# Transformer block on one core: when FFN weights are loaded, how late broadcasts land in the planner's model, and the order of the prologue

## The chip, the cores and the metric

The kernel runs on one core of one Trainium2 chip. The time is device time of one launch in microseconds (us), the median of several runs. One launch under the profiler gives the trace from which all durations below are taken. Engines are named as in the profile: PE (TensorE matmul; PEld is its weight load), DVE (VectorE), ACT (ScalarE), POOL (GpSimd), SP (SyncE, which here only issues DMAs).

## What is computed

One transformer block with conditioned layer norms, 2048 tokens of width 512, 32 heads of width 16, a gated FFN of width 1792. Weights and activations are bf16.

```python
mod = (silu(c) @ w_mod).reshape(1, 6, 1, -1)      # sa, ca, ga, sb, cb, gb
h = layernorm(x) * (1 + ca) + sa
q, k, v = split(h @ wqkv)                         # 32 heads of 16
p = softmax(q @ k.T / 4)                          # per head, 2048 x 2048
x = x + ga * ((p @ v) @ wo)
h = layernorm(x) * (1 + cb) + sb
x = x + gb * ((gelu(h @ w_gate) * (h @ w_up)) @ w_down)
```

The scores of all heads have 32 x 2048 x 2048 elements, and each needs one exponential. That is the bulk of the work outside PE.

## The kernel before

**A recorder with a model of time.** The kernel is not written as a fixed list of instructions. While it is built, every operation goes through `rec` (L168), which finds its dependences, adds semaphore waits and books it in `model` (L245), an estimate of when each engine is free and when each result is there (`op.t1`). A transfer is there, by the model, 1600 ns after its issue, or when the transfers before it are through, plus its bytes at 350 B/ns, plus 1000 ns. `probe` (L274) asks when an operation could start. `stream` (L1033) uses these answers to put the operations of all engines in order: whatever can start soonest without holding up ACT goes next. The order within each engine is then fixed in the program; at run time an engine waits at an instruction whose inputs are not there, and so does all that is behind it on that engine. The places in the order thus depend on the model's times, and a change of any of them can move everything behind it.

**The stream.** Queries are cut into seven sets (`SETS`): two of 512 tokens, three of 256, two of 128. For every set there are eight units `qd` of four heads each. A unit is a row of items; an item is one bank of 512 score columns in PSUM (128 keys by 512 columns, or more keys by fewer queries). There are 2048 items in all, and `pos` counts them. PE writes the scores of three items (`qk`) into one half of six PSUM banks, and ACT takes the exponential of two or three banks in one instruction (E<-ps_sc, 1024 or 1536 columns). Some items go to DVE instead: `exp_vec` computes the exponential there in seven steps, one `dt<-ps_sc`, then `dx`, two multiplications and two scalings in f16 and a last combination. The planner gives an item to DVE only where the conditions at `if (('v', 3, 0) in self.have` hold, among them that fewer than `BACK` = 10 DVE steps are waiting and that DVE is free by its own model within 700 ns. PE then multiplies with V (`pv_round`, ps_pv<-E,vaug), where a column of ones in V also gives the sum of the exponentials.

**The reciprocals.** When a unit is through, `pv_done` copies the sums and outputs to SBUF (`osb`), marks the unit in `self.live`, and sends the denominators round: to DRAM (`da`, scr_den<-osb), back in 128 partitions (`db`, den<-scr_den), a reciprocal on DVE (`fin1`), to DRAM (`dc`, scr_rec<-rden), and back as a broadcast over 32 partitions for each of four heads (`dd`, rb<-scr_rec, 256 KB for a set of 512). `fin2` on DVE multiplies (onorm<-osb,rb) and takes the unit out of `self.live`. All four transfers are issued by SP, in program order, each after its wait. For the first two units, which are interleaved, both sets of transfers come close together. 47 broadcasts are made this way; the last four units get their reciprocals on PE and DVE.

**Side work.** While the exponentials run, PE, DVE and, for the tanh of GELU, ACT also do the projections of K, V and Q (`side_k`, `side_v`, `side_q`), the modulation columns (`side_mod`), the output projection (`side_wo`) and the FFN of the sets that are through (`side_ffn`). `plan` gives each its stretch of positions; a `credit` paces it. DVE steps are queued as `task`s; a task made by `evac` goes first.

**FFN weights.** `weight_parts` makes a list of twelve transfers of the FFN weights, 448 KB for w_gate and w_up and mostly 512 KB for w_down. In `stream`, each is issued on SP once the second modulation (`modB`) is there, one every eight positions (`loaded = pos + 8`). The last two parts of w_up lie where DVE keeps its exponentials in the first set, and are put back to the list after `ends[0]`. They are in SP's program order with the transfers of the reciprocals.

**The prologue.** In `prologue`, SP and ACT issue the first loads. ACT's queue has x tiles 0 and 1 (`x0`), then tiles 4 to 7 (`x2`, 512 KB), then two thirds of the first weight columns (`wq0`, `wq2`), then tiles 12 to 15 (`x4`). SP's queue has c, tiles 2 and 3 (`x1`), the first third of w_mod (`wm0`, 1 MB), `wq1`, tiles 8 to 11 (`x3`), the other columns of wqkv and the rest of w_mod. DVE computes mean and variance of tiles 0 to 3 (`ln_stat`: bn_stats and bn_aggr), POOL one power for all four (`ln_rstd(0, 4)`), DVE then normalises them. ACT sums tiles 4 and 5 (`act_stat`: a Copy and a Square, each with an accumulator), which three small DVE operations (`act_stat_fin`) turn into mean and variance. PE computes the modulation columns (`mod_cols`, which needs `wm0`), transposes the normalised tiles, and projects K and Q of the first 512 tokens, after which the first exponential can start. At its end the prologue does `ln_stat` of tiles 6 and 7. `side_first` then goes on with V of the first 512 tokens, and with layer norm, transposes, K and V of the other three groups of 512; group 1 (tiles 4 to 7) is the first of these.

Of the kernel before, what the change touches and what calls it, by code (L numbers as in the profile page):

```python
# [5 lines left out]
ACT = mybir.ActivationFunctionType  # L6
# [8 lines left out]
P = 128  # L15
S_TOK = 2048
D = 512
# [61 lines left out]
class _Recorder:  # L79
# [282 lines left out]
    def bn_aggr(self, out, in_):  # L362
        return self.rec("dve", lambda e: e.bn_aggr(out, in_), [in_], [out], cost=90)

    def dma(self, eng, out, in_, sem, noncontig=False):
        def fn(e):
            if noncontig:
                with self.nc.allow_non_contiguous_dma(reason="small strided transfer"):
                    return e.dma_start(out, in_)
            return e.dma_start(out, in_)  # L370
        n = mybir.dt.size(out.dtype)
        for _, k in out.ap:
            n *= int(k)
        return self.rec(eng, fn, [in_], [out], dma=sem, cost=n)

    def emit(self, final):
        for s in self.count:
# [34 lines left out]
class _Kernel(_Recorder):  # L412
# [12 lines left out]
    def alloc(self):  # L425
        sb, ps = self.sb, self.ps
        self.xs = sb("xs", [P, NT, D], BF16)
        self.qT = sb("qT", [P, NDC, S_TOK], BF16)
        self.km = [sb("kme", [P, NDC, S_TOK], BF16), sb("kmo", [P, NDC, S_TOK], BF16)]
        self.vaug = sb("vaug", [P, NKT, H * VW], BF16)  # L430
        hreg = sb("hreg", [P, NDC * S_TOK], BF16)
        self.hT = hreg[:, :].rearrange("p (a n) -> p a n", a=NDC)
        self.prodT = hreg[:, 0:NFC * 512].rearrange("p (f n) -> p f n", f=NFC)
        self.tb2 = hreg[:, 0:4 * D].rearrange("p (t n) -> p t n", t=4)
        wreg = sb("wreg", [P, NDC * 1536], BF16)
        self.wqkv = wreg[:, :].rearrange("p (a n) -> p a n", a=NDC)
        self.t2T = wreg[:, 0:NDC * 512].rearrange("p (a n) -> p a n", a=NDC)
        self.gw = wreg[:, 2048:6144].rearrange("p (b k n) -> p b k n", b=2, k=2)
        mreg = sb("mreg", [P, 2 * NDC * F], BF16)
        self.wmod = mreg[:, 0:NDC * 3072].rearrange("p (a n) -> p a n", a=NDC)  # L440
        self.wg = mreg[:, 0:NDC * F].rearrange("p (a n) -> p a n", a=NDC)
        self.wu = mreg[:, NDC * F:2 * NDC * F].rearrange("p (a n) -> p a n", a=NDC)
        dreg = sb("dreg", [P, NFC * D], BF16)
        self.wd = dreg[:, :].rearrange("p (f n) -> p f n", f=NFC)
        self.tb1 = dreg[:, 0:8 * D].rearrange("p (b t n) -> p b t n", b=2, t=4)
        self.warm = dreg[:, 8 * D:9 * D]
        self.wo = sb("wo", [P, 8, D], BF16)
        self.E = sb("E", [P, NSL, 512], BF16)
        self.dt = [sb("dt%d" % i, [P, 512], I32)[:, :] for i in range(ND)]
        self.dlo = [t.bitcast(U16).rearrange("p (n t) -> p n t", t=2)[:, :, 0] for t in self.dt]  # L450
        self.dx = [sb("dx%d" % i, [P, 512], FP16)[:, :] for i in range(ND)]
        own = [sb("ed%d" % i, [P, 512], BF16)[:, :] for i in range(NED - 4)]
        c = NDC * 3072
        self.ED = [own + [mreg[:, c + 512 * i:c + 512 * i + 512] for i in range(4)],
                   own + [self.qT[:, i, 0:512] for i in range(4)]]
        self.onorm = sb("onorm", [P, 8, 512], BF16)
        self.ga = sb("ga", [P, D], BF16)
        self.gb = sb("gb", [P, D], BF16)
        self.xw = sb("xw", [P, D], BF16)
        self.osb = sb("osb", [P, 1024], FP32)  # L460
        self.rb = sb("rb", [P, 1024], FP32)
        self.den = sb("den", [P, 4, 16], FP32)
        self.rden = sb("rden", [P, 4, 16], FP32)
        self.mv = sb("mv", [P, NT, 2], FP32)
        self.st6 = sb("st6", [P, 2, 6], FP32)
        self.rstd = sb("rstd", [P, NT], FP32)
        self.nwt = sb("nwt", [P, NT], FP32)
        self.crow = dreg[:, 9 * D:10 * D]
        self.tcol = sb("tcol", [P, NDC], FP32)
        self.asum = sb("asum", [P, 2, 6], FP32)  # L470
        self.half = sb("half", [P, 4], FP32)
        self.sc_bf = sb("sc_bf", [P, NDC], BF16)
        self.scbc = sb("scbc", [P, NDC, P], BF16)
        self.modA = sb("modA", [P, 8], FP32)
        self.modB = sb("modB", [P, 8], FP32)
        self.rm4 = sb("rm4", [P, 4], FP32)
        self.rm = sb("rm", [P, 2], FP32)
        self.ident = sb("ident", [P, P], BF16)
        self.ones = sb("ones", [P, P], BF16)
        self.self32 = sb("self32", [P, P], FP32)  # L480
        self.scp = ps("ps_sc", [P, SC, 512], FP32)
        self.pv = ps("ps_pv", [P, 512], FP32)
        self.mi = ps("ps_mi", [P, 512], FP32)
        self.scr1 = self.dram("scr_den", [4, 2048], FP32)
        self.scr2 = self.dram("scr_rec", [4, 2048], FP32)


    def prologue(self):
# [6 lines left out]
        self.dma(act, self.xs[:, 0:2, :], xv[:, 0:2, :], "x0")  # L495
        self.dma(sp, self.xs[:, 2:4, :], xv[:, 2:4, :], "x1")
        self.dma(sp, self.wmod[:, :, 0:1024], wmv[:, :, 0:1024], "wm0")
        self.dma(act, self.xs[:, 4:8, :], xv[:, 4:8, :], "x2")
        for k in range(3):
            self.dma(sp if k == 1 else act, wq4[:, :, k, 0:P], wqv[:, :, k, 0:P], "wq%d" % k)  # L500
        self.dma(sp, self.xs[:, 8:12, :], xv[:, 8:12, :], "x3")
        self.dma(act, self.xs[:, 12:16, :], xv[:, 12:16, :], "x4")
        for k in range(3):
# [20 lines left out]
            self.mm(self.scp[:, 0, dc:dc + 1], self.crow[0:1, P * dc:P * dc + P], self.ones[0:1, 0:1])  # L524
        self.warm_up(16)
        self.act(self.tcol[:, :], self.scp[:, 0, 0:NDC], ACT.Tanh, scale=0.5)
        for t in range(4, 6):
            self.act_stat(t)
        for t in range(2):
            self.ln_stat(t)  # L530
        self.stt(self.tcol[:, :], self.tcol[:, :], 1.0, self.scp[:, 0, 0:NDC], ALU.add, ALU.mult)
        self.ts(dve, self.sc_bf[:, :], self.tcol[:, :], 0.5, None, ALU.mult)
        for t in range(2, 4):
            self.ln_stat(t)
        self.ln_rstd(0, 4)
        self.mod_cols(self.scp[:, 1, 0:8], 0)
        self.warm_up(2)
        for t in range(4):
# [10 lines left out]
        self.act(self.km[0][:, 0, 0:512], bank, ACT.Copy, scale=self.rm[:, 0:1])  # L549
        self.proj_q(0, 0, self.scp[:, 4, :], dve)  # L550
        self.ts(dve, self.km[1][:, 0, 0:512], bank, self.rm[:, 1:2], None, ALU.mult)
        for t in range(6, 8):
            self.ln_stat(t)
        self.act_stat_fin(4, 6)

    def act_stat(self, t):
        self.act(self.xw[:, :], self.xs[:, t, :], ACT.Copy, accum=self.asum[:, 0, t - 4:t - 3])
        self.act(self.xw[:, :], self.xs[:, t, :], ACT.Square, accum=self.asum[:, 1, t - 4:t - 3])

    def act_stat_fin(self, a, b):  # L560
        m, q, t = self.asum[:, 0, a - 4:b - 4], self.asum[:, 1, a - 4:b - 4], self.nwt[:, a:b]
        self.ts("dve", self.mv[:, a:b, 0], m, 1.0 / D, None, ALU.mult)
        self.stt(t, m, 1.0 / D, self.mv[:, a:b, 0], ALU.mult, ALU.mult)
        self.stt(self.mv[:, a:b, 1], q, 1.0 / D, t, ALU.mult, ALU.subtract)

    def warm_up(self, n):
        for _ in range(n):
# [117 lines left out]
    def side_first(self):  # L685
        def stats(tiles):
            for t in tiles:
                self.task([lambda t=t: self.ln_stat(t)], ("st", t))

        def norms(t0):  # L690
            g = t0 // 4
            self.task([("pool", lambda: self.ln_rstd(t0, t0 + 4))]
                      + [lambda t=t: self.ln_norm(t0 + t, self.tb1[:, g % 2, t, :]) for t in range(4)], ("ln", g),
                      self.after([("st", t) for t in range(max(8, t0), t0 + 4)]))
        if not self.dry:
            norms(4)
        yield from self.side_v(0, 0)
        if not self.dry:
            stats([8, 9, 10, 11])
            norms(8)  # L700
            stats([12, 13, 14, 15])
        for g in range(1, 4):
            yield from self.until(("ln", g))
            for h in range(2):
                yield from self.side_t(("a", g), lambda t: self.tb1[:, g % 2, t, :], 4, h,
                                       lambda dc: self.hT[:, dc, 512 * g:512 * g + 512], self.modA)
            if g == 1 and not self.dry:
                norms(12)
            yield from self.side_k(g, 0)
            yield from self.side_v(g, 0)  # L710
# [322 lines left out]
    def stream(self):  # L1033
# [64 lines left out]
        while pos < nseq:  # L1098
            if pos >= ends[0] and all(rof[v] < rp for v in low):
                parts, late = parts + late, []  # L1100
            while parts and "modB" in self.have and pos >= loaded:
                parts.pop(0)()
                loaded = pos + 8
            t = max(self.pe_now(), virt)
# [171 lines left out]
    def pv_done(self, rnd, acc):  # L1276
# [20 lines left out]
        def fin1():  # L1297
            self.recip(rden, den)
            self.dma("sp", s2.rearrange("(p n) -> p n", p=P), rden, "dc%d" % sem)
            self.dma("sp", self.rb[:, lo:hi],  # L1300
                     s2.rearrange("(j o n) -> j o n", j=4, o=1).broadcast_to([4, 32, W]), "dd%d" % sem)

        def fin2():
            c = OCOL[sets[0]]
# [176 lines left out]
```

## Time and profile before

| | us |
|---|---|
| runs (three): median, lowest, highest | 906.48, 906.29, 910.97 |
| the profiled execution | 907.0 |
| its span, first to last instruction | 905.3 |
| busy in the span: ACT | 876.5 |
| busy in the span: DVE | 817.4 |
| busy in the span: PE | 796.2 |
| busy in the span: POOL | 16.2 |

The span leaves out 1.7 us that the time of the launch has around it. The granted clock is 1.000 throughout. The views of the profile give times from the span's start. In a row of the timeline, the brackets at its end show how long the engine sat idle before it and what ended that wait; rows are merged where the same group follows itself without a gap worth telling. In a row of waits stand the engine that waited, its result and line, what it waited for, the sum, the count and the longest. L320, L324, L332, L337, L341 and L307 are helpers (`act`, `tt`, `ts`, `stt`, `copy`, `mm`), so groups are told apart by the names of tiles, where a region has the name of its tensor: mreg and qT and ed also hold DVE's exponentials, wreg the FFN's gate, dreg w_down and the normalised tiles, hreg the transposed ones.

### The profile page before, as it was taken

How to read it: one execution, taken by the hardware profiler on the slowest of the kernel's cores; microseconds unless marked ns; L12 is line 12 of the kernel's file. 1: busy time of each engine (PE TensorE's matmuls, PEld its weight loads, DVE VectorE, ACT ScalarE, POOL GpSimd, SP SyncE). 2: the span in 40 equal slices, each digit the busy share in tenths (PEclk: the TensorE clock that was granted, in tenths of full speed). 3: DMA queues.
4: the chain of work that ended last, by engine and by line, in shares of the span. 5: the costliest groups of instructions: out<-in, count | busy, mean ns of one | idle time of the engine just before them, and what ended most of it. 6: DMA issues, size and time to landing. Idle time of an engine off the chain costs nothing.

```text
span 905.3 us, 20373 instructions
## 1 busy us (share of the span) xinstructions
PE 796.2 (88%) x8565; PEld 291.3 (32%) x8700; DVE 817.4 (90%) x1976; ACT 876.5 (97%) x744; POOL 16.2 (2%) x34
## 2 busy tenths in 40 slices
PE   8898988888888889888898888998888998998888
PEld 3333322322222222222233323333433343234455
DVE  7687999999998999999998999999899899978955
ACT  6999999999999999999999999999999999999993
POOL 2100000000000000000000000000000000000000
PEclk9999999999999999999999999999999999999999
DMA  9012220000100000000000000010000000000000
GB/s 302 2 25 90 84 71 13 14 14 13 54 14 4 11 13 14 14 4 23 19 26 14 9 14 11 11 32 14 14 14 14 20 14 8 27 14 9 17 19 13
DMA packets 32514, 25.15 MB, mean 28 GB/s; under 512 B 16233, under 2 KB 28262, under 8 KB 32422
## 3 DMA queue, kind: packets, MB, share of 16 engines
q1 hardware_dynamic: 30038, 22.27, 8.2%
q10 hardware_dynamic: 2384, 1.57, 0.6%
q8 instruction: 68, 1.11, 0.5%
q14 instruction: 24, 0.20, 0.1%
HBM read 21.23 MB, written 2.61 MB: 26 GB/s over the span
## 4 chain that ended last, share of the span: by engine, by line
ACT 74%; DVE 11%; PE 8%; DMA 5%; issue 1%; POOL 0%
ACT E L320 72%; PE ps_sc L307 4%; DMA rb<-scr_rec 4%; PE ps_mi L307 3%; ACT wreg L320 2%; DVE dt L332 2%; DMA scr_rec<-rden 2%; PE ps_pv L307 1%; DVE qT L332 1%; DVE dx L332 1%; DVE ed L324 1%; DVE ed L337 1%; DVE qT L324 1%; DVE qT L337 1%; DVE mreg L324 0%
## 5 line engine op out<-in xcount | busy, mean ns | idle before, releaser
L320 ACT ACTIVATE E<-ps_sc 128x1536 bf16<-128x1536 f32 (+2 forms) x698 | 849.2, 1425 | 12.5 <-PE ps_sc L307 12.1
L307 PE MATMUL ps_sc<-qT,kme 32*128 32x256 bf16 (+2 forms) x1600 | 170.2, 304 | 20.6 <-ACT E L320 13.2
L307 PE MATMUL ps_sc<-qT,kmo 32*128 32x256 bf16 (+2 forms) x1664 | 168.4, 298 | 17.3 <-ACT E L320 12.8
L307 PE MATMUL ps_pv<-E,vaug 128*17 128x256 bf16 (+2 forms) x2906 | 181.2, 300 | 1.7 <-DVE vaug L341 0.8
L332 DVE TENSOR_SCALAR dt<-ps_sc 128x512 int32<-128x512 f32 x189 | 129.8, 688 | 8.9 <-PE ps_sc L307 6.4
L307 PE MATMUL ps_sc<-kme,ident 128*128 128x512 bf16 x299 | 96.3, 384 | 39.0 <-ACT E L320 33.4
L307 PE MATMUL ps_mi<-wreg,mreg 128*128 128x256 bf16 (+2 forms) x605 | 115.8, 306 | 5.9 <-DVE wreg L337 2.2
L307 PEld LDWEIGHTS ps_sc<-qT,kme 32*128 32x128 bf16 x1600 | 48.9, 92 | 128.6 <-ACT E L320 73.9
L307 PEld LDWEIGHTS ps_sc<-qT,kmo 32*128 32x128 bf16 x1664 | 50.2, 92 | 119.3 <-ACT E L320 68.0
L307 PEld LDWEIGHTS ps_pv<-E,vaug 128*17 128x17 bf16 x2906 | 52.9, 88 | 97.7 <-issue 85.9
L324 DVE TENSOR_TENSOR qT<-qT,dx 128x512 f16<-128x512 f16 x190 | 77.9, 419 | 1.0
L332 DVE TENSOR_SCALAR dx<-dt 128x512 f16<-128x512 uint16 x189 | 77.2, 419 | 0.1
L307 PEld LDWEIGHTS ps_mi<-wreg,mreg 128*128 128x128 bf16 x624 | 48.7, 97 | 57.1 <-issue 26.5
L337 DVE SCALAR_TENSOR_TENSOR qT<-dt,qT 128x512 int16<-128x512 int32 x95 | 65.0, 685 | 0.5
L307 PE MATMUL ps_mi<-dreg,hreg 128*128 128x512 bf16 x179 | 56.8, 384 | 3.7 <-issue 2.2
L324 DVE TENSOR_TENSOR ed<-ed,dx 128x512 f16<-128x512 f16 x128 | 52.4, 419 | 0.5
L307 PEld LDWEIGHTS ps_sc<-kme,ident 128*128 128x128 bf16 x331 | 23.4, 97 | 88.5 <-ACT E L320 84.9
L337 DVE SCALAR_TENSOR_TENSOR ed<-dt,ed 128x512 int16<-128x512 int32 x64 | 43.7, 686 | 0.4
L341 DVE CAST wreg<-ps_mi 128x512 bf16<-128x512 f32 x51 | 35.1, 689 | 9.6 <-PE ps_mi L307 8.7
L307 PE MATMUL ps_mi<-hreg,wreg 128*128 128x512 bf16 x101 | 32.8, 384 | 4.7 <-DVE qT L332 2.5
L337 DVE SCALAR_TENSOR_TENSOR wreg<-wreg,ps_mi 128x512 bf16<-128x512 bf16 x51 | 34.8, 683 | 2.2 <-ACT wreg L320 1.1
L307 PE MATMUL ps_pv<-qT,vaug 128*17 128x256 bf16 (+2 forms) x166 | 36.1, 290 | 0.0
(130 smaller groups left out, 739.0 us busy)
## 6 DMA issues: line engine op xcount, KB each, us to landing
rb<-scr_rec SPq DMA_DIRECT2D x16, 256.0 KB
rb<-scr_rec SPq DMA_DIRECT2D x29, 128.0 KB
mreg<-in_w_mod_dram SPq DMA_DIRECT2D x1, 2048.0 KB, 14.4
out_dram<-xs SPq DMA_DIRECT2D x16, 128.0 KB, 1.7
mreg<-in_B_w_gate_dram SPq DMA_DIRECT2D x4, 448.0 KB, 7.6
mreg<-in_B_w_up_dram SPq DMA_DIRECT2D x4, 448.0 KB, 7.1
dreg<-in_B_w_down_dram SPq DMA_DIRECT2D x3, 512.0 KB, 7.0
wreg<-in_A_wqkv_dram SPq DMA_DIRECT2D x3, 384.0 KB, 10.6
```

What stands on the lines that cost most here:

```text
L307: return self.rec("pe", lambda e: e.matmul(out, lhsT, rhs, start=start, stop=stop, tile_position=tp), [lhsT, rhs], [out], cost=(n, int(rhs ...
L320: return self.rec("act", lambda e: e.activation(out, in_, func, scale=scale, **kw), rd, wr, cost=self.cost("act", out, [in_], "act" if bia ...
L324: return self.rec(eng, lambda e: e.tensor_tensor(out, a, b, op), [a, b], [out], cost=self.cost(eng, out, [a, b], "tt"))
L332: return self.rec(eng, lambda e: e.tensor_scalar(out, a, s1, s2, **kw), rd, [out], cost=self.cost(eng, out, [a], "ts" if len(rd) == 1 else ...
L337: return self.rec("dve", lambda e: e.scalar_tensor_tensor(out, a, s, b, op0=op0, op1=op1), rd, [out], cost=self.cost("dve", out, [a, b], " ...
L341: return self.rec(eng, lambda e: e.tensor_copy(out, in_), [in_], [out], cost=self.cost(eng, out, [in_], "ts"))
```

## The change

Four edits, all in the building of the program:

- `dma` takes a number `late`, which is added to the model's landing time of that one transfer. The broadcast `dd` gets 3.5 ns for each query of its width and, up to the fifth set, 1000 ns more: 2792 ns for width 512, 1896 ns for width 256 in the sets three to five, 896 ns for the pair of the last two sets, 448 ns for width 128. No instruction is added by it; the waits stay as they are; what moves is where the planner puts what depends on it.
- An FFN weight transfer is put into the program only while `self.live` is empty, that is, while no unit stands between `pv_done` and `fin2`.
- `ln_rstd` of tiles 0 to 3 is done in two pairs. The first pair's power no longer waits for the statistics of tiles 2 and 3.
- Tiles 4 to 7 (`x2`) move from ACT's queue, where they were second, to SP's queue behind `wq1`. ACT's sums of tiles 4 and 5 are dropped with their three DVE operations; the statistics of tiles 4 to 7 become four tasks at the start of `side_first`, of two DVE instructions each, in place of those of tiles 6 and 7 at the end of the prologue. `norms(4)` now waits for all four of them by name.

```diff
-    def dma(self, eng, out, in_, sem, noncontig=False):
+    def dma(self, eng, out, in_, sem, noncontig=False, late=0):
...
-        return self.rec(eng, fn, [in_], [out], dma=sem, cost=n)
+        op = self.rec(eng, fn, [in_], [out], dma=sem, cost=n)
+        if op is not None:
+            op.t1 += late
+        return op
...
-        self.dma(act, self.xs[:, 4:8, :], xv[:, 4:8, :], "x2")
         for k in range(3):
             self.dma(sp if k == 1 else act, wq4[:, :, k, 0:P], wqv[:, :, k, 0:P], "wq%d" % k)
+        self.dma(sp, self.xs[:, 4:8, :], xv[:, 4:8, :], "x2")
         self.dma(sp, self.xs[:, 8:12, :], xv[:, 8:12, :], "x3")
...
-        for t in range(4, 6):
-            self.act_stat(t)
         for t in range(2):
             self.ln_stat(t)
+        self.ln_rstd(0, 2)
...
         for t in range(2, 4):
             self.ln_stat(t)
-        self.ln_rstd(0, 4)
+        self.ln_rstd(2, 4)
...
-        for t in range(6, 8):
-            self.ln_stat(t)
-        self.act_stat_fin(4, 6)
...
-                      self.after([("st", t) for t in range(max(8, t0), t0 + 4)]))
+                      self.after([("st", t) for t in range(t0, t0 + 4)]))
         if not self.dry:
+            stats([4, 5, 6, 7])
             norms(4)
...
-            while parts and "modB" in self.have and pos >= loaded:
+            while parts and "modB" in self.have and pos >= loaded and not self.live:
...
             self.dma("sp", self.rb[:, lo:hi],
-                     s2.rearrange("(j o n) -> j o n", j=4, o=1).broadcast_to([4, 32, W]), "dd%d" % sem)
+                     s2.rearrange("(j o n) -> j o n", j=4, o=1).broadcast_to([4, 32, W]), "dd%d" % sem, late=3.5 * W + (1000 if sets[0] < NS - 2 else 0))
```

The functions `act_stat` and `act_stat_fin` and the tiles `nwt` and `asum` go with their last use.

More of the change, by code (lines that the diff above doesn't have):

```diff
@@ L466, in alloc @@
         self.rstd = sb("rstd", [P, NT], FP32)
-        self.nwt = sb("nwt", [P, NT], FP32)
         self.crow = dreg[:, 9 * D:10 * D]
         self.tcol = sb("tcol", [P, NDC], FP32)
-        self.asum = sb("asum", [P, 2, 6], FP32)
         self.half = sb("half", [P, 4], FP32)
@@ L551, in prologue @@
         self.ts(dve, self.km[1][:, 0, 0:512], bank, self.rm[:, 1:2], None, ALU.mult)
-        for t in range(6, 8):
-            self.ln_stat(t)
-        self.act_stat_fin(4, 6)
[L556 to L564, printed above, removed]
     def warm_up(self, n):
```

## The prediction

> **What bounds the kernel now.** First the page's busy shares: ACT is busy for 97% of the span, so the time can fall only where ACT idles or where it gets less to do. Then the windows, to see where it idles.
>
> ```profile
> PE 796.2 (88%) x8565; PEld 291.3 (32%) x8700; DVE 817.4 (90%) x1976; ACT 876.5 (97%) x744; POOL 16.2 (2%) x34
> ```
> ```profile
> 0.00:15.00 15.00, 11.74 (x87) 5.21 (x88) 8.64 (x26) 6.49 (x13) 4.65 (x13) 1.00 0.93 285
> ...
> 75.00:150.00 75.00, 66.00 (x554) 21.60 (x563) 68.36 (x169) 73.67 (x61) 0.00 (x0) 1.00 0.26 78
> ...
> 230.00:270.00 40.00, 34.91 (x247) 9.25 (x250) 37.58 (x95) 39.07 (x33) 0.00 (x0) 1.00 0.12 35
> ...
> 590.00:620.00 30.00, 26.92 (x333) 9.39 (x333) 27.89 (x73) 28.84 (x25) 0.00 (x0) 1.00 0.10 27
> ```
>
> The fourth pair of numbers in a row is ACT. Three stretches hold most of its idle time between prologue and tail: 75.00 - 73.67 = 1.33, 40.00 - 39.07 = 0.93 and 30.00 - 28.84 = 1.16, together 3.42 us. The row at the top says that nearly all of the first 15 us goes by before the first exponential. Next the waits, for what happens in the three stretches, and the chain of waits with its times:
>
> ```profile
> DVE onorm L324 <- DMA rb<-scr_rec: 10.4, 9, 2.0
> ```
> ```profile
> 83.16 6.26 DMA rb<-scr_rec
> ...
> 110.17 2.47 DMA scr_rec<-rden
> 112.66 6.22 DMA rb<-scr_rec
> ...
> 135.46 1.41 DMA scr_rec<-rden
> 136.88 5.18 DMA rb<-scr_rec
> ...
> 240.93 6.50 DMA rb<-scr_rec
> ```
>
> DVE stands nine times, 10.4 us in all, at `fin2` until a broadcast has landed, and the chain runs through those transfers in the same stretches where ACT idles. What stands behind `fin2` on DVE are the steps of exponentials, the first of which frees the score bank that PE needs next and ACT after it. That is how a late transfer reaches ACT; most of the 10.4 us are taken up by the banks in hand before they get there (3.42 of idle against 10.4 of waiting).
>
> Two causes can be told apart in these rows. At 135 us, with no weights under way, the way back takes 1.41 + 5.18. In the stretches with weights it is 6.26, 6.22 and 6.50 for the broadcast, 1.0 to 1.3 more, and once 2.47 for the small transfer ahead of it, 1.06 more. SP's timeline has the weights right behind the broadcast (its first row is `wm0`, for later):
>
> ```profile
> 1.69 0.45 SPq L370 DMA_DIRECT2D mreg<-in_w_mod_dram  x1
> ...
> 83.74 2.06 SPq L370 DMA_DIRECT2D mreg<-in_B_w_gate_dram  x4
> ...
> 103.68 0.52 SPq L370 DMA_DIRECT2D scr_den<-osb  x1
> ...
> 129.57 0.52 SPq L370 DMA_DIRECT2D scr_den<-osb  x1
> ```
>
> But also the undisturbed broadcast takes longer than the planner has it: 256 KB are 1600 + 749 + 1000 ns = 3.35 us in its model, against 5.18. So `fin2` is put about 1.8 us too early on DVE even without weights.
>
> **The change, part by part.** *Gate.* It adds no instruction and moves twelve weight transfers. In the first set a unit ends every 26 us (103.68, 129.57) and is out for some 13 (129.57 to 136.88 + 5.18 = 142.06), so about 13 us are left free, which is three transfers at one every eight positions (2048 items in 865 us are 0.42 us each, eight 3.4). The ten parts of the first list need three or four such pauses and are through by about 170 us. The two late ones go behind the broadcast that ends at 240.93 + 6.50 = 247.4. By the plan the FFN of the first set starts 93 positions (39 us) after the set's end, whose broadcast this is, so near 270: cover of some 20 us for two transfers; were it gone, PE would stand for one landing. On SP nothing is queued behind a weight transfer any longer but the next unit's transfers. I take the gate as worth the 1.0 to 2.1 us by which the disturbed broadcasts were late, in each of the three worst waits.
>
> By the Trainium skill, page "DMA: Bandwidth & Descriptors", section "Queues, rings and completion order", descriptors of one issuing queue are consumed in ring order on each DMA engine, so weights issued behind a broadcast on SP could not hold it up. The row at 83.16 speaks against that (6.26 with weights only behind it, 5.18 without), and I go by the row; by the rule, the gate would help only the broadcasts with weights ahead of them and the sum would lose about 1 us.
>
> *Later landing in the model.* For width 512, 3.35 + 2.79 = 6.14 us: now above the 5.18 measured. `fin2` will be put where its data has landed, and up to 2.8 us of other DVE steps go before it. What is late next: `live` and the `onorm` tiles stay open longer, which the output projection waits for; it has its place 33 positions (14 us) after a set's end, so that a delay of 2 to 3 us is mostly inside its pacing.
>
> Both together: I take 0.8 of the 3.42 us of idle time as won, 2.7 us, since a new order will have small gaps of its own; bounds 0 (the idle shows up elsewhere) and 3.42.
>
> *DVE's time.* Of the 10.4 us, a part becomes room for more exponentials. Prices, by groups of instructions:
>
> ```profile
> L320 ACT ACTIVATE E<-ps_sc 128x1536 bf16<-128x1536 f32 x475 | 685.2, 1563 | 5.2 <-PE ps_sc L307 4.9
> L320 ACT ACTIVATE E<-ps_sc 128x1024 bf16<-128x1024 f32 x217 | 244.3, 1145 | 0.5 <-PE ps_sc L307 0.3
> ```
> ```profile
> L332 DVE TENSOR_SCALAR dt<-ps_sc 128x512 int32<-128x512 f32 x189 | 129.8, 688 | 8.9 <-PE ps_sc L307 6.4
> ...
> L332 DVE TENSOR_SCALAR dx<-dt 128x512 f16<-128x512 uint16 x189 | 77.2, 419 | 0.1
> ...
> L337 DVE SCALAR_TENSOR_TENSOR ed<-dt,ed 128x512 int16<-128x512 int32 x64 | 43.7, 686 | 0.4
> ...
> L324 DVE TENSOR_TENSOR ed<-ed,dx 128x512 f16<-128x512 f16 x128 | 52.4, 419 | 0.5
> ...
> L332 DVE TENSOR_SCALAR ed<-ed 128x512 f16<-128x512 f16 x64 | 18.0, 287 | 0.3
> ```
>
> A bank costs ACT 1563 - 1145 = 418 ns. On DVE it costs 688 + 419 + 2 x 287 + 2 x 419 + 686 = 3.2 us. Half of the 10.4 us would be 5.2 / 3.2 = 1.6 exponentials, 0.7 us of ACT. All of it would be 1.36 us; the other bound is a loss, below. The planner does not see run-time waits, so it need not use this room; half is a choice in the middle.
>
> *Prologue.* The wait that ends last before the first exponential is `mod_cols`, in the chain:
>
> ```profile
> 7.45 0.24 POOL rstd L578
> ...
> 7.76 1.06 POOL rstd L579
> ...
> 9.41 0.94 PE ps_sc L307 x32
> ```
> ```profile
> 8.85 1.38 DVE L332 TENSOR_SCALAR dreg<-xs,mv,rstd 128x512 bf16<-128x512 bf16 x4 [1.49 <-POOL rstd L579]
> ...
> 10.64 1.05 PE L311 MATMUL ps_sc<-ident,dreg 128*128 128x128 bf16 x16
> ...
> 15.26 25.20 ACT L320 ACTIVATE E<-ps_sc 128x1536 bf16<-128x1536 f32 x22 [1.36 <-PE ps_sc L307]
> ```
>
> The second fence is the timeline of all engines: normalising, transposes, first exponential. What `mod_cols` (9.41) needs is `wm0`, issued at 1.69 us. The DMA view, in the window 4.2 to 5.4 us (packets by queue) and for `wm0`:
>
> ```profile
> DMA packets 436, 0.46 MB, mean 381 GB/s; under 512 B 12, under 2 KB 414, under 8 KB 436
> ...
> q10 hardware_dynamic: 414, 0.41, 98.2%
> q1 hardware_dynamic: 22, 0.05, 12.2%
> ```
> ```profile
> mreg<-in_w_mod_dram SPq DMA_DIRECT2D x1, 1024.0 KB, 7.6
> ```
>
> 1.69 + 7.6 = 9.3: `wm0` lands just ahead of `mod_cols`. In the window ACT's queue (q10) has nearly all packets, and they are x tiles 4 to 7; `wm0` on SP's queue (q1) hardly moves. Without these 512 KB ahead, at 381 GB/s, it lands 1.38 us earlier. The other leg is the power. In pairs:
>
> ```profile
> L579 POOL TENSOR_TENSOR rstd<-rstd,half 128x4 f32<-128x4 f32 x6 | 6.4, 1073 | 0.5
> L579 POOL TENSOR_TENSOR rstd<-rstd,half 128x2 f32<-128x2 f32 x3 | 2.3, 780 | 0.2
> ```
>
> The second pair's power ends at 7.76 + 0.78 = 8.54, and only two tiles are left to normalise instead of four, 2 x 0.35: done at 9.25 instead of 8.85 + 1.38 = 10.23. `mod_cols` ends at 9.41 + 0.94 - 1.38 = 8.97 plus the warm-up that follows (0.3 up to the transposes): 9.3. Both legs meet there, 1.3 us earlier than the transposes at 10.64. What ACT did for tiles 4 and 5 lay in its idle time and gives nothing. One extra pair of POOL instructions runs beside DVE's statistics: nothing. `x2` now takes the place of `x3` on SP and moves `x3`, the rest of wqkv and the rest of w_mod one issue (0.5 us) back, `x4` on ACT forward; its tiles should land at about 13 us (all loads share the rate, and what was ahead of `x3` is now ahead of it), and DVE turns to them at about 14. Were they later, group 1 would be, below.
>
> Some of the 1.3 us is given back at group 1, whose K is needed 32 items later. DVE's and PE's timelines:
>
> ```profile
> 27.67 0.75 DVE L332 TENSOR_SCALAR kme<-ps_mi,rm 128x512 bf16<-128x512 f32 x1
> ```
> ```profile
> 28.48 0.38 PE L307 MATMUL ps_sc<-qT,kme 32*128 32x512 bf16 x1
> ```
>
> K is ready at 28.42 and used at 28.48, so this road is tight now. DVE gets two more tiles of statistics ahead of group 1's power and loses three small operations:
>
> ```profile
> L360 DVE BATCH_NORM_STATS2 st<-xs 128x6 f32<-128x512 bf16 x10 | 6.8, 676 | 0.0
> ...
> L363 DVE BATCH_NORM_AGGREGATE mv<-st 128x2 f32<-128x6 f32 x9 | 1.6, 182 | 0.3
> ...
> L337 DVE SCALAR_TENSOR_TENSOR nwt<-asum,mv 128x2 f32<-128x2 f32 x1 | 0.2, 162 | 0.0
> ```
>
> 2 x (0.68 + 0.18) - 3 x 0.16 = 1.24 us more, which just eats the earlier start. Against that, DVE now does statistics of group 2 between group 1's power and its normalising, and these can go behind. I take 1.0 us as net; bounds: 1.3 won, and 1.2 lost if `wm0` does not come earlier and the statistics are in the way in full.
>
> **Sum.** -2.7 - 0.7 - 1.0 = -4.4 us on the profiled 907.0 gives 902.6; its own time stands 0.5 above the median 906.48, so the median should come to **902.1**. About 0.5% is what a measurement of this kernel can tell from no change: faster than 901.95 is called faster, above 911.0 slower. The forecast thus lies on the edge.
>
> **Rivals.** *The idle only moves.* The planner's order is new from 20 us on; if the order has as many gaps as now, what stays is the prologue: 906.5 - 1.0 = 905.5. For it: only 3.42 of 10.4 us of waiting reached ACT, so the tie is loose. Against: the chain runs through broadcasts in the first two stretches, which hold most of the idle time.
>
> *The queues share, and `wm0` comes no earlier.* ACT's queue still holds `wq0`, `wq2` and `x4`, 768 KB, beside it. If both queues drain side by side whatever was issued, the prologue gives nothing: 903.1. Against it speak the 22 packets of 436, with `wm0` issued 2.5 us before that window. By the same page and section of the Trainium skill, a DMA engine takes turns between the queues that have work, packet by packet; that would be this case, and the trace agrees only once both queues are under way.
>
> *All of it comes.* 3.42 idle + 1.36 in exponentials + 1.3 prologue = 6.1: 900.4.
>
> *Fewer exponentials on DVE: the slow side.* Its place is the planner's choice of items for DVE. With the later landing, `fin2` waits among the tasks for 1.9 to 2.8 us longer, per unit of 13 to 27 us, takes up one of the ten places in the backlog, and pushes other steps into it when it comes. Each exponential that stays on ACT costs 0.418 us, and nothing hides it. From 4.4 / 0.418 = 11 fewer of 189 on the change is a loss; 22 fewer would be 906.5 - 4.4 + 9.2 = 911.3. For it: DVE is 90% busy and the condition bites often. Against: the same work is in DVE's list, and its run-time waits fall.
>
> **How the numbers follow.** Forecast 0.45 (its own range 900.3 to 904.0), idle moves 0.13, queues share 0.08, all of it 0.20, fewer exponentials 0.14. Faster by over 0.5%: all of the fourth and over half of the first, 0.46. Slower by over 0.5%: two thirds of the last, 0.09. The rest is 0.45. The range goes from 899.0 (1.4 us, three exponentials, below "all of it") to 907.2, which leaves out most of the slow case and a little below.
>
> **What would show it.** Right: the row of DVE's onorm waiting for rb falls from 10.4 us to under 3; in the windows, ACT idles under 1 us in all of the three stretches; weights in SP's timeline stand only between an onorm and the next scr_den; the first E starts at about 14 us instead of 15.26, and `mod_cols` near 8.1. Wrong: `mod_cols` still at 9.4; E rows with an idle of over 0.5 us near 27 us; the count of `dt` under 180; new rows in which PE waits for a weight transfer after 270 us; rb waits gone with ACT's idle unchanged.

## The result and the profile after

The changed kernel takes 901.85 us (median of 6 runs, 901.01 to 902.43) against 906.5 of the kernel before beside it (6 runs, 905.21 to 910.97): a ratio of 0.9941, 95% interval 0.9921 to 0.9962. Its profiled execution took 902.15 with a span of 900.3, 5.0 us less than the span of before. Where single executions are compared below: the granted clock averages 0.994 to 1.000 over one of them, and the kernel before has a median of 905.54 in 19 executions at 1.000 and of 907.04 in 10 below it.

Where the 5.0 us come from is in the windows of the changed kernel (columns as before; the fourth pair is ACT):

```profile
0.00:15.00 15.00, 12.29 (x88) 5.34 (x88) 8.59 (x26) 3.59 (x5) 5.36 (x15) 1.00 0.94 284
...
75.00:150.00 75.00, 68.79 (x583) 22.36 (x584) 71.97 (x174) 74.76 (x63) 0.00 (x0) 1.00 0.27 77
...
230.00:270.00 40.00, 36.84 (x265) 9.91 (x263) 38.98 (x100) 40.00 (x34) 1.28 (x2) 1.00 0.14 38
...
590.00:620.00 30.00, 28.55 (x353) 9.19 (x352) 29.32 (x75) 30.00 (x26) 0.00 (x0) 1.00 0.10 29
```

In the three stretches ACT now idles 0.24, 0 and 0 us instead of 1.33, 0.93 and 1.16: 3.2 of the 5.0 us. DVE is busier in each of them, because it no longer stands at `fin2`. The view of the tile onorm lists what DVE was idle for before its instructions (sum, times):

```profile
  DMA rb<-scr_rec: 0.3, 1
```

That was 10.4 us in nine waits. The chain of waits of the changed kernel, by engine, has lost its transfers; before, its shares were ACT 74%, DVE 11%, DMA 5%:

```profile
ACT 91%; PE 6%; DVE 1%; DMA 1%; issue 0%; SPq 0%
```

The rest lies in ACT's busy time. From 15 us on it is 871.55 - 3.59 = 867.96 us against 876.48 - 6.49 = 869.99, 2.0 less (the two together are 0.2 over the 5.0; small gaps elsewhere make the difference). One exponential more went to DVE, worth 0.42 by the price of a bank:

```profile
L332 DVE TENSOR_SCALAR dt<-ps_sc 128x512 int32<-128x512 f32 x190 | 129.9, 686 | 9.3 <-PE ps_sc L307 6.9
```

The other 1.6 us are in exponentials that take the same number of instructions less busy time. The page's row of E has 698 in both kernels: 849.2 us busy before, and now

```profile
L320 ACT ACTIVATE E<-ps_sc 128x1536 bf16<-128x1536 f32 (+2 forms) x698 | 847.5, 1434 | 9.4 <-PE ps_sc L307 9.1
```

The cause can be counted in the traces. Consecutive exponentials overlap: one of 1536 columns that begins before the one ahead of it is through ends 1343 ns after that one (median), and one that begins only afterwards takes 1451 ns. With 1024 columns it is 917 and 1024. So each exponential that gets its scores too late to overlap costs some 0.11 us of busy time beside the idle gap. There are 27 of them before and 13 after the change, which is 14 x 0.11 = 1.5 us. The stalls cost more than the idle time showed.

Two things did not come as the names of the edits say. SP's timeline has weights directly behind each broadcast, as before:

```profile
83.37 0.54 SPq L370 DMA_DIRECT2D rb<-scr_rec  x1
83.97 1.93 SPq L370 DMA_DIRECT2D mreg<-in_B_w_gate_dram  x4
102.93 0.52 SPq L370 DMA_DIRECT2D scr_den<-osb  x1
...
112.31 0.53 SPq L370 DMA_DIRECT2D rb<-scr_rec  x1
112.88 0.95 SPq L370 DMA_DIRECT2D mreg<-in_B_w_up_dram  x2
```

And the prologue ends where it ended. `mod_cols`, first exponential and group 1's K, in the timelines of PE, ACT and DVE of the changed kernel:

```profile
9.46 0.94 PE L307 MATMUL ps_sc<-sc_bf,mreg 128*128 128x1 bf16 x32 [0.55 <-DMA mreg<-in_w_mod_dram]
...
15.31 3.71 ACT L320 ACTIVATE E<-ps_sc 128x1536 bf16<-128x1536 f32 x3 [1.36 <-PE ps_sc L307]
...
27.84 0.75 DVE L332 TENSOR_SCALAR kme<-ps_mi,rm 128x512 bf16<-128x512 f32 x1
```

against 9.41, 15.26 and 27.67.

### The profile page after: what moved, and what is told of

Read it like the earlier page. It is cut to its first block, busy times and chain, and to the rows that moved or that the text cites. A ratio compares the mean times of both kernels' runs of the same rounds, so it can differ in the third digit from the quotient of the medians.

```text
span 900.3 us, 20502 instructions
## 1 busy us (share of the span) xinstructions
PE 821.3 (91%) x8704; PEld 290.0 (32%) x8704; DVE 820.9 (91%) x1984; ACT 871.5 (97%) x736; POOL 17.2 (2%) x36
## 3 DMA queue, kind: packets, MB, share of 16 engines
q8 instruction: 68, 1.11, 0.6%
## 4 chain that ended last, share of the span: by engine, by line
ACT 91%; PE 6%; DVE 1%; DMA 1%; issue 0%; SPq 0%
ACT E L320 89%; PE ps_sc L307 3%; ACT wreg L320 3%; PE ps_mi L307 2%; PE ps_pv L307 1%; DMA mreg<-in_w_mod_dram 1%; DVE st L360 0%; ACT hreg L320 0%; DVE qT L332 0%; DVE wreg L337 0%; DVE qT L324 0%; SPq L370 0%; DVE xw L324 0%; DVE dt L332 0%; PE ps_sc L311 0%
## 5 line engine op out<-in xcount | busy, mean ns | idle before, releaser
L307 PE MATMUL ps_sc<-qT,kme 32*128 32x256 bf16 (+2 forms) x1600 | 167.6, 304 | 12.4 <-ACT E L320 8.4
L307 PE MATMUL ps_sc<-kme,ident 128*128 128x512 bf16 x349 | 112.1, 384 | 41.4 <-ACT E L320 39.3
L307 PE MATMUL ps_mi<-wreg,mreg 128*128 128x256 bf16 (+2 forms) x624 | 120.8, 308 | 4.4 <-DVE wreg L337 1.7
L307 PE MATMUL ps_mi<-dreg,hreg 128*128 128x512 bf16 x210 | 65.3, 385 | 1.1 <-DVE xw L324 0.6
L307 PE MATMUL ps_mi<-hreg,wreg 128*128 128x512 bf16 x120 | 37.5, 385 | 0.4 <-DVE vaug L341 0.2
## 6 DMA issues: line engine op xcount, KB each, us to landing
mreg<-in_w_mod_dram SPq DMA_DIRECT2D x1, 2048.0 KB, 12.5
```

The lines of the kernel that those rows point to most:

```text
L307: return self.rec("pe", lambda e: e.matmul(out, lhsT, rhs, start=start, stop=stop, tile_position=tp), [lhsT, rhs], [out], cost=(n, int(rhs ...
```

## The experiments

Theory A: the planner put `fin2` too early on DVE; the later landing in its model takes the wait away, and the gate and the prologue do little. Rival B: the waits were made by weights beside the broadcasts, and the gate took them away. Rival C: any new order may win or lose such an amount by chance.

### One edit at a time

`only_late` is the kernel before with `late` and nothing else.

> The kernel before with the later landing alone. Theory A (the planner put fin2 too early; with the landing corrected DVE no longer stands there): DVE's wait of onorm for rb falls from 10.4 us to under 1.5, ACT idles under 0.6 us in all between 75 and 150, 230 and 270, 590 and 620 us, time 901.5 to 903.5. Rival B (the wait was made by weights that travel beside the broadcasts, and the gate takes it away): waits of 3 us or more stay, time above 904.5. Rival C (the gain is a lucky new order): no gain that goes with the wait.

Measured: 901.83 us (901.81 to 902.99), before 905.8 beside it, ratio 0.9959 (0.9947 to 0.9971). No row of DVE waiting for rb is left, and the windows are those of the changed kernel:

```profile
75.00:150.00 75.00, 69.05 (x586) 22.61 (x586) 71.97 (x174) 74.76 (x64) 0.00 (x0) 1.00 0.25 77
230.00:270.00 40.00, 36.84 (x264) 9.98 (x263) 38.98 (x99) 40.00 (x35) 1.36 (x2) 1.00 0.13 38
590.00:620.00 30.00, 28.40 (x356) 9.05 (x349) 29.39 (x76) 30.00 (x26) 0.00 (x0) 1.00 0.09 29
```

Within the noise this edit alone is the whole result: the changed kernel has 0.9941 (0.9921 to 0.9962).

`only_gate` adds the gate alone:

```diff
-            while parts and "modB" in self.have and pos >= loaded:
+            while parts and "modB" in self.have and pos >= loaded and not self.live:
```

> The kernel before with the gate on the weights alone. Theory A: SP still issues weights right behind a broadcast, since nothing at run time makes SP wait for fin2; DVE's wait for rb stays at 7 us or more, time 905 to 907.5. Rival B: the wait falls under 4 us, time under 904.

Measured: 906.02, ratio 1.0002 (0.9994 to 1.0011). The order of the program is the same as before on PE, DVE, ACT and POOL; on SP a few transfers have moved. The wait stays, and the chain of waits shows the slow broadcasts as they were:

```profile
DVE onorm L324 <- DMA rb<-scr_rec: 7.8, 7, 2.0
```
```profile
83.09 6.27 DMA rb<-scr_rec
...
110.12 2.32 DMA scr_rec<-rden
112.45 6.41 DMA rb<-scr_rec
...
135.43 1.41 DMA scr_rec<-rden
136.86 5.20 DMA rb<-scr_rec
```

`only_prol` has the new prologue alone.

> The kernel before with the new prologue alone. Theory A: mod_cols at 9.4 and the first exponential at 15.3 us as in both profiles, DVE's wait for rb stays at 8 us or more, time 905.5 to 907.5. Rival (the prologue gives the 1.0 us that the prediction had): time 904.5 to 905.7.

Measured: 906.27, ratio 1.0011 (1.0000 to 1.0022). The expectation of 9.4 and 15.3 us was wrong for its profiled execution, which is one where `wm0` did come early:

```profile
8.30 0.94 PE L307 MATMUL ps_sc<-sc_bf,mreg 128*128 128x1 bf16 x32
...
14.16 2.36 ACT L320 ACTIVATE E<-ps_sc 128x1536 bf16<-128x1536 f32 x2 [1.36 <-PE ps_sc L307]
```

That execution took 904.69 us, the lowest of the kernel's twelve, while the median gains nothing, and none at a clock of 1.000 alone either (905.86 in 7 executions, 905.54 in the 19 of the kernel before). The landing of `wm0` varies: 6.5, 6.9, 7.6 and 7.2 us after its issue in the four profiles with `x2` moved (`only_prol`, `no_late`, the changed kernel, `wm0_alone` below), 7.6 to 7.8 in seven of the eight without, and 8.6 in the eighth (`true_gate` below).

`no_late` is the changed kernel without `late`.

> The changed kernel without the later landing (gate and new prologue stay). Theory A: back to 905.5 to 907.5, wait for rb 7 us or more. Rival B: 902 to 904, wait for rb under 4 us.

Measured: 906.36, ratio 1.0003 (0.9991 to 1.0015), wait for rb 6.7 us in six waits. Just under the 7 expected; the time is as theory A has it. Rival B's form, in which the gate of the change does it, falls here.

### A gate that holds at run time

`only_gate` leaves open whether weights slow a broadcast at all, since they still travelled beside it. `true_gate` is `only_gate` with a real wait: each weight transfer also reads, for the recorder, the onorm columns that the last `fin2` wrote.

```diff
+            self.rec("sp", lambda e: e.dma_start(dst, src), [src, self.lastn], [dst], dma=sem, cost=n)
...
             if self.probing is None:
+                self.lastn = self.onorm[:, qd, c:c + W]
                 self.live.pop(u)
```

> The kernel before with a gate that holds at run time: besides not being recorded while a unit is live, each weight transfer waits for the last fin2. The order on PE, DVE and ACT is that of the kernel before. If weights behind a broadcast slow it (the prediction's view): the broadcasts at 83, 112 and 242 us take 5.2 instead of 6.2 to 6.5, DVE's wait for rb falls from 7.8 (gate alone) to 4 to 6 us, time 0.3 to 1.5 us under the gate alone. If they take what they take without weights too: the same 6.2 to 6.5, wait 7 us or more, time as with the gate alone within 0.5.

Measured: 903.0 us (12 runs), before 906.65, ratio 0.9964 (0.9952 to 0.9976), with the order of PE, DVE and ACT of the kernel before. SP's timeline has the weights some 6 us behind the broadcast now, and the chain gives that broadcast's landing:

```profile
114.39 0.53 SPq L370 DMA_DIRECT2D rb<-scr_rec  x1
120.37 0.33 SPq L760 DMA_DIRECT2D mreg<-in_B_w_up_dram  x1
```
```profile
111.93 2.45 DMA scr_rec<-rden
114.39 5.23 DMA rb<-scr_rec
```
```profile
75.00:150.00 75.00, 67.98 (x567) 21.65 (x569) 70.18 (x172) 74.75 (x62) 0.00 (x0) 1.00 0.23 78
230.00:270.00 40.00, 36.55 (x266) 9.37 (x258) 38.94 (x96) 39.72 (x33) 0.00 (x0) 1.00 0.11 36
590.00:620.00 30.00, 27.71 (x329) 9.35 (x331) 27.77 (x75) 28.75 (x25) 0.00 (x0) 1.00 0.10 30
```

The broadcast takes 5.23 instead of 6.41 us, and the other two, from issue to the last update of their semaphore, 5.00 and 4.89 instead of 6.27 and 6.41. The wait for rb falls from 7.8 to 5.0 us, and ACT idles only 0.25 and 0.28 us in the two stretches with weights. So weights behind a broadcast do slow it, and holding them back was worth more than the 0.3 to 1.5 us expected: 3.0 us between the two medians, 3.4 by their ratios (1.0002 and 0.9964), since the runs of before beside them differ by 0.85. At a clock of 1.000 alone it is 2.5 against the kernel before (902.80 in 8 executions, 905.34 in 7).

In the third stretch no weights travel. ACT idles 1.25 us there, 1.16 before, but only 0.25 in `only_gate`, with one order of PE, DVE and ACT in all three. The chain of waits before has a slow small transfer there:

```profile
604.08 3.56 DMA scr_rec<-rden
607.65 3.52 DMA rb<-scr_rec
```

In `true_gate` the same transfer takes 3.56 too, in `only_gate` 1.39. Beside it each trace has one packet of 16 KB on the instruction queue (q8 in the DMA view of a page). It starts 1.11 us after the transfer's issue before, 1.10 in `true_gate` and 1.28 in `only_gate`. In the first two, fifteen of the transfer's sixteen semaphore updates are there by 1.39 us and the last comes 1.1 us after that packet's end; in `only_gate` the last comes 0.1 us after the packet's start, 1.39 after the issue, as without any packet. So this stall came from neither the weights nor the model's landing time, but from a collision that one execution has and another has not. The changed kernel's profile has it as well (3.50 for the transfer issued at 599.00). There the broadcast is in by 605.9 and `fin2`, which the model now puts 1.9 us later in the sets of width 256, runs at 607.3, so DVE does not wait.

What the gate of the change lacked is the wait: the recorder puts weights behind `fin2` in its own time, but on SP the next thing in front of them is the broadcast's issue, and SP goes on as soon as that is out.

### How late

`late_half` and `late_double` are `only_late` with `late` halved and doubled.

> The kernel before with half of the later landing (1396 ns for width 512, 948 for 256). Theory A: by the model 3.35 + 1.40 = 4.75 us against 5.2 to 6.5 measured, so a part of the waits stays, 1 to 5 us, and the time lies between: 902.5 to 905. Rival C (any new order has the gain or not by chance): wait and time do not go together.

> The kernel before with twice the later landing (5584 ns for width 512, 3792 for 256). Theory A: no wait for rb is left, as with the later landing alone, and nothing more is won: 901 to 903. If the longer life of a unit costs something (a full backlog, a later output projection), 903 or more with fewer than 187 exponentials on DVE.

Measured: 902.78 (0.9950, 0.9933 to 0.9967) with 1.2 us of waiting for rb left, and 902.53 (0.9958, 0.9942 to 0.9973) with none and 191 exponentials on DVE. With `only_late` these are three different orders, all with the wait small or gone, all at 901.8 to 902.8: chance (rival C) would hardly make such a row, and `true_gate` gained with the order of the kernel before. Doubling is 0.7 us above `only_late` in the median, within the intervals, so a longer life of a unit costs little here, if anything.

`late_true` and `half_true` put the gate that holds on the full and the half later landing, again with the order of PE, DVE and ACT unchanged against those.

> The kernel before with the later landing and the gate that holds at run time; the order on PE, DVE and ACT is that of the later landing alone. If the later landing already hides the collisions (no wait for rb was left with it alone): nothing more, 901.5 to 902.3, wait for rb under 0.5 us. If the collisions cost something besides that wait: under 901.2.

> The kernel before with half of the later landing and the gate that holds at run time; the order on PE, DVE and ACT is that of half the later landing alone (wait for rb 1.2 us there). If the two act on the same wait from its two sides: wait under 0.5 us, 901.7 to 902.7. If they add up: 900 or less.

Measured: 902.03 (0.9953, 0.9937 to 0.9969) and 901.76 (0.9950, 0.9934 to 0.9966), with 0.3 and 0.2 us of waiting for rb left, once each. The two act on one wait from its two sides: the one lets the data come earlier, the other lets DVE ask later. No version is clearly below the changed kernel.

### What holds `wm0`

`wm0_alone` is the changed kernel with `wq0`, `wq2` and `x4` also on SP's queue, behind `wm0`; ACT's queue has `x0` alone.

> The changed kernel with all first weight columns and x tiles 4 to 15 behind wm0 on SP's queue, so that ACT's queue has x0 alone. If the other queue's transfers hold wm0 back (queues share): wm0 lands by 7.6 us, the first exponential starts at 14.1 to 14.4, where the normalising ends last, and the time is 0.7 to 1.2 us under the changed kernel, 900.6 to 901.2. If wm0's landing is set by one late DMA engine whatever else runs: mod_cols between 8.3 and 9.6 as in the runs so far, time as the changed kernel within 0.5.

Measured: 901.95 us (0.9946, 0.9929 to 0.9963); `wm0` lands 7.2 us after its issue, `mod_cols` starts at 9.22, the first exponential at 15.08. By its numbers that is the second case expected. It does not clear the other queue, though: `wq0`, `wq1` and `wq2` now stand right behind `wm0` on its own queue, and loads behind a broadcast on one queue were seen to slow it (6.41 against 5.23). More can be read from the sixteen semaphore updates of `wm0`. Before, all come 7.0 to 7.6 us after its issue. In the changed kernel fifteen come at 5.9 to 6.5, and the last at 7.64. In `wm0_alone` eight are there by 5.84, and the last comes at 7.16. In the window 5 to 7 us the two queues moved, in the kernel before and then in the changed kernel (packets, MB):

```profile
q1 hardware_dynamic: 287, 0.59, 81.1%
q10 hardware_dynamic: 297, 0.15, 25.8%
```
```profile
q1 hardware_dynamic: 352, 0.70, 94.9%
q10 hardware_dynamic: 135, 0.03, 7.8%
```

Before, the two queues move nearly as many packets each; with `x2` out of the way SP's queue moves most. So the x tiles did hold `wm0` back, by about 1.1 us, and moving them did speed up the bulk of it; yet the landing row reads 7.6 in both, because one of the sixteen updates came late in the changed kernel. In `no_late` two came late, by less (6.9), and in `only_prol` none. No packet of the instruction queue runs at that time. What makes such an update late was not tried and stays open.

## Why the prediction was right, point by point

The predicted 902.1 and the measured 901.85 agree, and part of that is luck. The prologue's 1.0 is missing in the result and the gate gave nothing, while the later landing alone gave what it, the gate and the exponentials were to give together, and a little more (3.7 against 3.4), in part through a term that the sum did not have. The kernel before, from which the prediction counted, ran 906.5 in the runs beside the result and 905.8 in the 29 beside the first experiments.

- *What bounds the kernel.* Right: ACT's idle time in the three stretches hung on DVE's waits for broadcasts, and went with them. The third had another source than the prediction's two causes: there a packet of the instruction queue made the transfer ahead of the broadcast late (3.56 us instead of 1.39).
- *Later landing, and DVE's time.* The sum had 2.7 + 0.7 = 3.4 us for the gate, the later landing and room for exponentials. The later landing alone gives 905.8 x 0.0041 = 3.7 (interval 2.6 to 4.8). The room went less to exponentials (one instead of 1.6) than to exponentials that overlap again (1.5 us, a term that the sum did not have).
- *Gate.* The step that failed is "On SP nothing is queued behind a weight transfer any longer but the next unit's transfers", and with it the forecast that weights stand only between an onorm and the next scr_den. A place in the recorded order is not a time on an engine that has nothing to wait for there. The gate alone is worth 1.0002; the price put on it, 1.0 to 2.1 us per disturbed broadcast, was about right for the broadcast itself (6.41 to 5.23), and it is the gate with a wait that gets it. The small transfer's 1.06 us was wrongly booked to the weights: in `only_gate` it takes 2.32, in `true_gate` 2.45, with no weights under way. Here too a packet of the instruction queue runs beside it (last section).
- *The ring-order rule.* Weighed against the row at 83.16, the row was the right choice. By the Trainium skill, page "DMA: Bandwidth & Descriptors", section "Queues, rings and completion order", descriptors are consumed in ring order on each DMA engine, though a later one may finish its write before an earlier one. That weights could therefore not hold up a broadcast ahead of them was the prediction's own inference, and the traces do not bear it out: 6.41 with weights behind it, 5.23 without.
- *Prologue.* The step that failed is "Without these 512 KB ahead, at 381 GB/s, it lands 1.38 us earlier". It did by 1.1 in the profile of `only_prol`. In that of the changed kernel fifteen of its sixteen updates did (6.51 against 7.57 us after the issue), but not the last, with which it lands (7.64 against 7.59), so that `mod_cols` at 9.46 is one of the prediction's own signs of being wrong. In the medians the term of 1.0 is 0 (1.0011 for the prologue alone). The other leg was right: normalising ended at 8.56 + 0.74 = 9.30 in the changed kernel, 9.25 predicted, as its timeline shows:

```profile
8.56 0.74 DVE L332 TENSOR_SCALAR dreg<-xs,mv,rstd 128x512 bf16<-128x512 bf16 x2 [0.61 <-POOL rstd L566]
```

- *Group 1's K.* The fear that more statistics make it late did not come true: it is 12.5 us behind the first exponential after the change (27.84 - 15.31) and was 12.4 before.
- *Rivals.* Fewer exponentials on DVE: no, 190. The idle only moves: no. All of it comes (900.4): no, the prologue's part is missing. Queues share: its time of 903.1 would have been near, but not its mechanism, since most of `wm0` did come earlier.

## What to carry to other kernels

Where a planner writes the order of an in-order engine, an optimistic time for one slow transfer costs all that is queued behind its consumer; compare the model's time with the landing in the trace, and correct that first, with some room for landings that vary (one number in the model was the whole 0.4 to 0.6% here). A transfer that is to keep out of another's way needs a wait at run time; a place further down in the program does nothing on a queue that has no reason to stop. And price a transfer that decides a start by several executions: it has landed with the last of its semaphore updates, and here one of sixteen alone was up to 2.2 us late.

## What the runs showed of the hardware that was not expected

- Loads of 448 or 512 KB issued right behind a 256 KB broadcast on the same queue slow it. In the twelve profiles it takes 5.9 to 6.9 us with two to six loads behind it (28 broadcasts), 5.2 to 5.3 with one (3), and 4.6 to 5.3 with none (161).
- The 1 MB load at the start landed 6.5 to 8.6 us after its issue in the twelve profiles. In those of the changed kernel and of `true_gate` fifteen of its sixteen updates were there 1.1 us before the last (6.51 and 7.64; 7.49 and 8.63).
- The profile of `true_gate` also shows a granted clock of 0.91 in the first 15 us, that of `late_half` 0.89. From the start of `mod_cols` to the first exponential both take 6.9 us, against 5.9 in the ten profiles at 1.00. With the late load, the first exponential of `true_gate` starts at 17.37; the execution took 906.47 us against its kernel's median of 903.0:

```profile
0.00:15.00 15.00, 12.00 (x83) 5.43 (x84) 7.73 (x24) 6.15 (x13) 4.65 (x13) 0.91 0.93 285
```

- A transfer of 8 KB takes 2.2 to 3.1 us near 110 us and 1.4 at 135, whether weights are under way or not. In all twelve profiles fifteen of its sixteen updates are there by 1.4 us. The last comes 1.0 to 1.1 us after the end of a 16 KB packet of the instruction queue that starts 0.1 to 1.1 us after the transfer's issue (before: packet from 110.55 to 111.54, last update at 112.64). It looks as if a sixteenth of the transfer stood behind that packet on one DMA engine; the traces do not say which engine a packet ran on.
